# PV of both halves in the next step, and preparation in small pieces: attention and two expert layers on one core

## The chip, the cores and the metric

The program runs on one core of a Trainium2 chip. The metric is the device time of one execution in microseconds (us); 1592.23 us is the median of three runs of the kernel before (1590.58 to 1593.88). The engines are named as the profile names them: PE (TensorE's matmuls), PEld (its weight loads), DVE (the vector engine), ACT (the scalar engine), POOL and SP (which issues nearly all DMAs).

## The reference

Three parts follow one another. Attention: 8 batches, 8 heads, 576 tokens, head size 64, with a mask by blocks of 64:

```python
scores = 1/np.sqrt(64) * (q @ k.transpose(0, 1, 3, 2))
scores = np.where(block_i >= block_j, scores, -1e9)      # blocks of 64 tokens
attn = exp(scores - max); attn = attn / (attn.sum(-1) + 1e-09)
x = (attn @ v) as 4608 tokens x 512
```

Then a gated layer, `h = ((x @ w1) * (x @ w2)) @ w3 @ w_out`, with w1 and w2 of 512 x 1024, w3 of 1024 x 1024, w_out of 1024 x 512. Then routing: `logits = h @ w_gate` for 8 experts, each token given in the order of all logits to the best expert that still has room (576 tokens each), and `relu(h @ w1[e]) @ w2[e]` of its expert. The gated layer's w1, w2, w3 and w_out arrive as float64 and are decoded to float32 on the chip (`decode`); the rest is float32.

## The kernel before

Products are made in float16 pairs: a value is scaled by a power of two and split into a high and a low half (`split`: ACT writes the high half, DVE the low one), and three of the four products are summed in PSUM (`PRODUCTS`). The scale comes from a sum of squares (`ssq` on ACT), summed over partitions by a matmul with ones (`total`, PE), and a few tiny DVE operations (`pow2`).

The attention stage is a loop over 32 steps (`step`), one for each pair of heads n of batch n // 4. A step has four score tiles in PSUM (`s_tiles`): `last` (64 query tokens of both heads), and `rows` for 128-token blocks 3, 2 with 0, and 1. For each, PE makes the scores into S; DVE takes the row maximum (nb); ACT takes the exponential (E) with its sum; DVE takes the reciprocal; ACT or DVE writes the high half of P and DVE the low half (`finish`). `last` and block 3 fill one SBUF tile of P (13 blocks wide, PT13 when transposed), the rest another (12 wide, PT12). When such a tile is full, `transP` issues two DMA transposes on SP, one a half, into one buffer each. `pv(n, part)` multiplies the transposed tile with v: part 0 is PT13 (54 matmuls), part 1 PT12 (36). Both use the single PSUM bank named PV, which ACT and DVE evict into xT (`pv`'s last lines); the w34 products of the weights use the same bank.

Into the list of a step's work are woven the step's fills (`interleave`): the decoding, scaling and splitting of w1 and w2 (`do_w`, steps 1 to 7), the chunks of w_out (steps 8 to 11) with `wo_split` and `wo_dot` (step 12), w3 and `w34` (steps 14 to 31), and from step 5 on four `moe_unit`s a step. A unit is 24 matmuls of 288 columns into two `ab` banks: ACT evicts the first as a_sb, DVE multiplies it with the second to g, and SP stores two of them (gd).

The preparation of a step's inputs stands between its score tiles: at odd n `prep_qk` (squares of q and k, `total`, scale, both splits, and the copy q4 for `last`) and the load of the next q and k; at n divisible by 4 `scale_v` (squares of a batch's v); at even n `prep_v` (the split of v for two steps, 1280 columns).

The code gives only an order of priority. The framework's scheduler sets the order on each engine: it goes through the list by priority and by when its own model finds an instruction's inputs ready. From the route on (`manual_schedule`) the order of PE, ACT and POOL is written out. So the same lines may come out elsewhere in an engine's stream than they stand in the code. In the sections below, a tile's name with a number is one buffer of that name.

Of the kernel before, what the change touches and what calls it, by code (L numbers as in the profile page):

```python
# [27 lines left out]
OSTEP = 8  # L28
# [31 lines left out]
def moe_kernel(ctx, tc, q, k, v, moe_w1, moe_w2, moe_w3, moe_w_out, w_gate, ew1, ew2, out):  # L60
# [14 lines left out]
    def pow2(pool, m, name, TB=TB, inv=None, **kw):  # L75
        n = m.shape[-1]
        t = pool.tile([P, 3, n], I32, name=name, **kw)
        nc.vector.tensor_scalar(t[:, 0], m.bitcast(I32), 24, 23, op0=ALU.logical_shift_right,
                                op1=ALU.logical_shift_left)
        nc.vector.tensor_scalar(t[:, 1], t[:, 0], -1.0, float((189 + TB) << 23), op0=ALU.mult, op1=ALU.add)  # L80
        if inv is not None:
            nc.gpsimd.tensor_scalar(inv.bitcast(I32), t[:, 0], float((65 - TB) << 23), 0.0, op0=ALU.add, op1=ALU.add)
            return t[:, 1].bitcast(F32), None
        nc.vector.tensor_scalar(t[:, 2], t[:, 0], float((65 - TB) << 23), None, op0=ALU.add)
        return t[:, 1].bitcast(F32), t[:, 2].bitcast(F32)
# [31 lines left out]
    def split(hi, lo, x, s):  # L117
        nc.scalar.activation(hi, x, AF.Copy, scale=s)
        nc.vector.scalar_tensor_tensor(lo, x, s, hi, op0=ALU.mult, op1=ALU.subtract)
# [5 lines left out]
    def ssq(x, dst, junk):  # L125
        nc.scalar.activation(junk, x, AF.Square, accum_out=dst)
# [8 lines left out]
    def load_v(b):  # L135
        nc.sync.dma_start(v32, v[b])

    def scale_v(b):
        m = sm.tile([P, 3], F32, name="vm")
        vhl[4 * b] = c2.tile([P, 2, 4, 5, D], F16, name="v16")  # L140
        j = vhl[4 * b].rearrange("p z h j d -> p (z h) j d")
        for x in range(3):
            ssq(v32[:, :, 2 * x:min(2 * x + 2, 5), :], m[:, x:x + 1], j[:, :, 2 * x:min(2 * x + 2, 5), :])
        m2 = total(m)
        m3 = sm.tile([P, 1], F32, name="vm3")
        nc.vector.tensor_reduce(m3, m2, axis=AX.X, op=ALU.add)
        sv[b] = pow2(sm, m3, "vp")

    def prep_v(n):
        b, hp = divmod(n, NP)  # L150
        vt = vhl[n] if n % 4 == 0 else c2.tile([P, 2, 4, 5, D], F16, name="v16")
        split(vt[:, 0], vt[:, 1], v32[:, 2 * hp:2 * hp + 4], sv[b][0])
        vhl[n], vhl[n + 1] = vt[:, :, 0:2], vt[:, :, 2:4]

    def scale_x(b):
        r = mo.tile([P, 8], F32, name="vr", bufs=2)
# [9 lines left out]
    def unscale(b, f):  # L166
        nc.vector.tensor_scalar(iv[b][:, f], iw12[:, f], ivs[b], ivs[b], op0=ALU.mult, op1=ALU.mult)

    def prep_qk(g):
        n0, n1 = GROUPS[g]  # L170
        t, w = qk32.pop(g), n1 - n0
        m = sm.tile([P, 2], F32, name="qm")
        T = c2.tile([P, 2, 2, 2, S], F16, name="qkT")
        for z in range(2):
            ssq(t[:, z, :w], m[:, z:z + 1], T[:, z, 1, :w])
        s, e = pow2(sm, total(m), "qp")
        c = sm.tile([P, 2], F32, name="cc")
        for z, f in enumerate((1.0, -1.0)):
            nc.vector.scalar_tensor_tensor(c[:, z:z + 1], e[:, 0:1], f * 0.125, e[:, 1:2],
                                           op0=ALU.mult, op1=ALU.mult)  # L180
        for z in range(2):
            split(T[:, z, 0, :w], T[:, z, 1, :w], t[:, z, :w], s[:, z:z + 1])
        for hh in range(2):
            r = slice(64 * hh, 64 * hh + 64)
            nc.vector.tensor_copy(q4[r, :, n0 % 2:n0 % 2 + w, r], T[r, 0, :, :w, 512:])
        for n in range(n0, n1):
            qkT[n] = T[:, 0, :, n - n0], T[:, 1, :, n - n0], q4[:, :, n % 2], c

    PRODUCTS = ((0, 0), (0, 1), (1, 0))

# [209 lines left out]
    def total(m):  # L400
        n = m.shape[-1]
        p = ps_l.tile([P, 512], F32, name="lgp")
        nc.tensor.matmul(p[:, :n], ones, m, start=True, stop=True)
        return p[:, :n]

    es_w = ExitStack()
    stg_w = es_w.enter_context(tc.tile_pool(name="stg_w", bufs=2))

    def prep_w(n, f):
        w = stg_w.tile([P, 512], F32, name="wd")  # L410
        decode((n, f), w)
        m = sm.tile([P, 1], F32, name="wm")
        t = w16[n][f].rearrange("p z c f -> p z (c f)")
        ssq(w, m, t[:, 1])
        e = scaled(w, total(m), t[:, 0], t[:, 1], "wp")
        nc.vector.tensor_copy(iw[n][:, f:f + 1], e)
        if n == "w2":
            nc.vector.scalar_tensor_tensor(iw12[:, f:f + 1], iw["w1"][:, f:f + 1], 2.0 ** 15, e, op0=ALU.mult, op1=ALU.mult)
# [28 lines left out]
    def wo_split():  # L447
        m2 = total(wo["m"])
        m3 = sm.tile([P, 1], F32, name="wom3", bufs=1)
        nc.vector.tensor_reduce(m3, m2, axis=AX.X, op=ALU.add)  # L450
        s, e = pow2(sm, m3, "wop")
        wo["e"] = e
        t = wo["t"]
        for c in range(8):
            w = wo["w"][:, c]
            split(t[:, c, 0], t[:, c, 1], w, s)
        wo["wg"], wo["eg"] = hilo(wo["g"], 4, "wgx")

    def wo_dot():
        wo["stack"].close()  # L460
# [76 lines left out]
            else:  # L537
                load_raw(x, wi[x[0]][x[1]])

    def do_w(n, f):  # L540
        prep_w(n, f)
        next_load()

    def do(f, *a):
        f(*a)
        next_load()
# [3 lines left out]
    load_v(0)  # L550
    prep_qk(0)
    prep_qk(1)
    for _ in range(2):
        next_load()
    scale_v(0)
# [4 lines left out]
    for n, m in WSTEP.items():  # L560
        for _ in range(m):
            x = next(ws)
            add(n, do_w, *x)
    for c in range(8):
        add(OSTEP + c // 2, do, wo_chunk, c)
    add(OSTEP + 4, wo_split)
    add(OSTEP + 4, wo_dot)
    for f in range(8):
        a, b_ = S3 + int(R3 * f), S3 + int(R3 * f + R3 / 2)
        add(a, do, w3_chunk, f, 0)  # L570
# [22 lines left out]
    def step(n):  # L593
        ops = []
        if n < NS:
            a, b_, c, d = s_tiles(n)
            pre = []
            if n % 2:
                g = first.get(n + 1)
                if g is not None:  # L600
                    pre.append(lambda: prep_qk(g))
                    if g + 1 < len(GROUPS):
                        pre.append(lambda: load_qk(g + 1))
            elif n == 0:
                pre.append(lambda: load_qk(2))
            if n % 4 == 0 and n:
                pre.append(lambda: scale_v(n // 4))
            if n % 2 == 0 and n:
                pre.append(lambda: prep_v(n))
            if n % 4 == 3 and n // 4 + 1 < B:  # L610
                pre.append(lambda: load_v(n // 4 + 1))
            ops += [a, lambda: (b_(), transP(n, 0))]
            ops += pre
            ops += [c, lambda: (d(), transP(n, 1))]
            if n:
                ops.insert(2, lambda: pv(n - 1, 1))
            ops.append(lambda: pv(n, 0))
        elif n == NS:
            ops.append(lambda: pv(n - 1, 1))
        if n % 4 == 0 and 0 < n <= NS:  # L620
            ops.append(lambda: scale_x(n // 4 - 1))
        interleave(ops, fills[n])
# [538 lines left out]
```

## Time and profile before

| | |
|---|---|
| median of three runs | 1592.23 us (1590.58 to 1593.88) |
| profiled execution, its time | 1593.24 us |
| profiled execution, span from first to last instruction | 1591.5 us |
| mean granted clock of TensorE | 0.944 |
| PE busy | 1376.4 us |
| DVE busy | 1024.5 us |
| ACT busy | 891.7 us |

Busy is the time in which an engine has at least one instruction under way. The granted clock is the share of TensorE's 2.4 GHz that the throttle let through; 0.5 is its lower level of 1.2 GHz. A row of waits names who waited, for whom, and the time in total, how often, and the longest. In a row of the timeline, the square bracket holds the idle time of the engine ahead of the row and what ended it.

### The profile page before, as it was taken

How to read it: one execution, taken by the hardware profiler on the slowest of the kernel's cores; microseconds unless marked ns; L12 is line 12 of the kernel's file. 1: busy time of each engine (PE TensorE's matmuls, PEld its weight loads, DVE VectorE, ACT ScalarE, POOL GpSimd, SP SyncE). 2: the span in 40 equal slices, each digit the busy share in tenths (PEclk: the TensorE clock that was granted, in tenths of full speed). 3: DMA queues.
4: the chain of work that ended last, by engine and by line, in shares of the span. 5: the costliest groups of instructions: out<-in, count | busy, mean ns of one | idle time of the engine just before them, and what ended most of it. 6: DMA issues, size and time to landing. Idle time of an engine off the chain costs nothing. (4 is left out here: it accounts for less than half of the span.)

```text
span 1591.5 us, 32778 instructions
## 1 busy us (share of the span) xinstructions
PE 1376.4 (86%) x12811; PEld 942.3 (59%) x12811; DVE 1024.5 (64%) x3068; ACT 891.7 (56%) x2121; POOL 98.0 (6%) x136
## 2 busy tenths in 40 slices
PE   3558887978998999999999888888768999989997
PEld 2335565656666666666666665656555656556663
DVE  8898888777788787874224888878743353343610
ACT  8887977577677677754322333353314564555721
POOL 0000000000000000100200000000023121200101
PEclk9557999999999999999999999989879999999999
DMA  8758796886768676469964434333258663642200
GB/s 266 185 146 173 187 221 119 186 186 136 168 161 202 155 183 120 93 119 249 295 202 148 127 101 133 100 113 100 100 112 187 177 201 133 123 175 74 80 27 34
DMA packets 379659, 238.57 MB, mean 150 GB/s; under 512 B 261232, under 2 KB 344688, under 8 KB 378480
## 3 DMA queue, kind: packets, MB, share of 16 engines
q1 hardware_dynamic: 372064, 215.47, 52.9%
q0 software_dynamic: 5760, 18.90, 4.0%
q10 hardware_dynamic: 1680, 2.11, 0.6%
q8 instruction: 100, 1.64, 0.4%
q14 instruction: 55, 0.45, 0.1%
HBM read 132.61 MB, written 39.86 MB: 108 GB/s over the span
## 5 line engine op out<-in xcount | busy, mean ns | idle before, releaser
L301 PE MATMUL ab<-xT,w1h 128*128 128x288 f16 x1536 | 223.0, 295 | 11.5 <-ACT a_sb L306 11.3
L301 PE MATMUL ab<-xT,w2h 128*128 128x288 f16 x1536 | 215.4, 289 | 7.7 <-DVE g L311 3.6
L1079 PE MATMUL pe<-xT,ewa 128*128 128x288 f16 (+2 forms) x1728 | 198.6, 279 | 16.8 <-DMA xT<-xg 9.4
L1079 PEld LDWEIGHTS <-ewa 128*128 128x128 f16 x1728 | 160.7, 101 | 53.5 <-DVE sc L1057 9.5
L1096 PE MATMUL pe<-ewb,h 128*128 128x512 f16 (+1 forms) x960 | 189.1, 379 | 0.0
L301 PEld LDWEIGHTS <-w1h 128*128 128x128 f16 x1536 | 147.1, 101 | 66.3 <-issue 24.4
L221 ACT ACTIVATE E<-S,nb,cc 128x128 f32<-128x128 f32 (+4 forms) x288 | 181.1, 637 | 2.8 <-DVE P L232 0.9
L301 PEld LDWEIGHTS <-w2h 128*128 128x128 f16 x1536 | 146.4, 99 | 53.3 <-issue 13.5
L232 DVE SCALAR_TENSOR_TENSOR P<-E,rr,P 128x128 f16<-128x128 f32 (+4 forms) x288 | 155.7, 573 | 13.7 <-ACT P L231 11.9
L276 PE MATMUL PV<-PT,v 128*64 128x128 f16 (+1 forms) x2880 | 100.7, 225 | 53.0 <-DMA PT<-P 45.7
L1096 PEld LDWEIGHTS <-h 128*128 128x128 f16 (+1 forms) x960 | 85.3, 101 | 99.2 <-issue 2.6
L276 PEld LDWEIGHTS <-v 128*64 128x64 f16 x2880 | 86.5, 120 | 75.8 <-issue 49.7
L1082 DVE SCALAR_TENSOR_TENSOR h<-pe,h 128x288 f16<-128x288 f32 (+2 forms) x144 | 57.2, 419 | 106.9 <-ACT h L1081 106.6
L922 PE MATMUL px<-W34l,gh 128*128 128x512 f32 x288 | 123.0, 427 | 0.0
L922 PE MATMUL px<-W34h,gh 128*128 128x512 f32 x288 | 122.0, 424 | 0.0
L937 ACT ACTIVATE gh<-g 128x1024 fp32r<-128x1024 f32 x36 | 38.1, 1059 | 149.8 <-PE px L922 142.6
L922 PE MATMUL px<-W34h,gl 128*128 128x512 f32 x288 | 121.9, 423 | 0.0
L311 DVE SCALAR_TENSOR_TENSOR g<-ab,vr,a_sb 128x288 f32<-128x288 f32 x124 | 63.5, 512 | 83.6 <-PE ab L301 73.6
L1081 ACT ACTIVATE h<-pe 128x288 f16<-128x288 f32 (+2 forms) x144 | 52.5, 380 | 111.7 <-PE pe L1079 110.1
L200 PE MATMUL S<-qkT 64*128 64x512 f16 (+3 forms) x768 | 83.7, 324 | 27.1 <-ACT E L221 26.3
L213 DVE TENSOR_REDUCE nb<-S 128x2 f32<-128x1024 f32 (+3 forms) x128 | 101.2, 814 | 7.5 <-PE S L204 7.4
L231 ACT ACTIVATE P<-E,rr 128x128 f16<-128x128 f32 (+3 forms) x176 | 97.2, 603 | 12.9 <-DVE rr L225 11.4
(279 smaller groups left out, 2173.3 us busy)
## 6 DMA issues: line engine op xcount, KB each, us to landing
g<-gd SPq DMA_DIRECT2D x36, 512.0 KB, 3.9
gd<-g SPq DMA_DIRECT2D x62, 288.0 KB, 2.9
g<-gd SPq DMA_DIRECT2D x15, 1152.0 KB, 7.2
raw<-in_moe_w_dram SPq DMA_DIRECT2D x32, 512.0 KB, 4.8
esa<-in_moe_w_dram SPq DMA_DIRECT2D x8, 2048.0 KB, 9.2
esb<-in_moe_w_dram SPq DMA_DIRECT2D x8, 2048.0 KB, 9.5
v<-in_v_dram SPq DMA_DIRECT2D x8, 1280.0 KB, 6.5
xr<-row SPq DMA_DIRECT2D x36, 256.5 KB, 3.0
```

What stands on the lines that cost most here:

```text
L200: nc.tensor.matmul(ps[:, hh, o:o + N], tq[r, a, m * P:m * P + P], tk[r, b, :N], start=a + b == 0, stop=False)
L213: nc.vector.tensor_reduce(nb[:, 0, k_:k_ + 2], ps[:, :, o:o + N], axis=AX.X, op=ALU.max)
L221: nc.scalar.activation(ef[:, a], pf_[:, a], AF.Exp, bias=nb[:, 1, x:x + 1], scale=c[:, 0:1], accum_out=sums[:, x:x + 1])
L231: nc.scalar.activation(hi, ef[:, at[x]], AF.Copy, scale=r[:, 1, x:x + 1])
L232: nc.vector.scalar_tensor_tensor(lo, ef[:, at[x]], r[:, 1, x:x + 1], hi, op0=ALU.mult, op1=ALU.subtract)
L276: nc.tensor.matmul(ps[hh * 64:hh * 64 + 64, c0:c0 + w], vt[:, zv, hh, j, :], s, start=z == 0 and j == 0, stop=z == 2 and j == nj - 1)
L301: nc.tensor.matmul(p[:, :288], w[:, zw, cc, :], x[:, zx, cc, c0:c0 + 288], start=first, stop=cc == 3 and zw == 1)
L311: nc.vector.scalar_tensor_tensor(g, ps["w2"][:, :288], iv[b][:, f:f + 1], a, op0=ALU.mult, op1=ALU.mult)
L922: nc.tensor.matmul(p, gh[a][:, f], W34[b][:, f], start=f == 0 and a + b == 0, stop=f == 7 and a == 1)
L1079: nc.tensor.matmul(p[:, :n], w1[:, a, cc, f * P:(f + 1) * P], t[:, 4 * b + cc, x], start=cc == 0 and a + b == 0, stop=cc == 3 and a == 1)
L1082: nc.vector.scalar_tensor_tensor(h[:, 1, f, x], p[:, :n], 0.0, h[:, 0, f, x], op0=ALU.max, op1=ALU.subtract)
L1096: nc.tensor.matmul(p[r0:r1], h[:, a, f, k_ * P + r0:k_ * P + r1], EW[e, "b"][0][:, b, f], start=f == 0 and a + b == 0, stop=f == 7 and a == 1)
```

## The change

Both halves of pv(n-1) are handed over in step n, the first behind `last`, the second behind the third score tile; before, the first half stood at the end of step n-1 and the second behind the second tile of step n. `prep_qk` is cut into squares and scale (at the even step before) and two splits (at the odd step). v is split for each step (640 columns) into four smaller buffers instead of for two steps (1280 columns) into two. The decoding of w1 and w2 (`dec_w`) and their split (`prep_w`) are two fills, and the next raw load is issued behind the first. The eight splits of w_out are fills of their own, in steps 12 and 13, and `wo_dot` moves to step 13. All pieces are dealt out between the step's score tiles.

```diff
     def scale_v(b):
         m = sm.tile([P, 3], F32, name="vm")
-        vhl[4 * b] = c2.tile([P, 2, 4, 5, D], F16, name="v16")
+        vhl[4 * b] = c2.tile([P, 2, 2, 5, D], F16, name="v16", bufs=4)
...
     def prep_v(n):
         b, hp = divmod(n, NP)
-        vt = vhl[n] if n % 4 == 0 else c2.tile([P, 2, 4, 5, D], F16, name="v16")
-        split(vt[:, 0], vt[:, 1], v32[:, 2 * hp:2 * hp + 4], sv[b][0])
-        vhl[n], vhl[n + 1] = vt[:, :, 0:2], vt[:, :, 2:4]
+        if hp:
+            vhl[n] = c2.tile([P, 2, 2, 5, D], F16, name="v16", bufs=4)
+        split(vhl[n][:, 0], vhl[n][:, 1], v32[:, 2 * hp:2 * hp + 2], sv[b][0])
...
+    pq = {}
+
+    def qk_scale(g):
+        n0, n1 = GROUPS[g]
+        w = n1 - n0
+
+        def sq(z):
+            if z == 0:
+                pq[g] = sm.tile([P, 2], F32, name="qm"), c2.tile([P, 2, 2, 2, S], F16, name="qkT")
+            m, T = pq[g]
+            ssq(qk32[g][:, z, :w], m[:, z:z + 1], T[:, z, 1, :w])
+
+        def fin():
+            m, T = pq[g]
+            s, e = pow2(sm, total(m), "qp")
+            c = sm.tile([P, 2], F32, name="cc")
+            for z, f in enumerate((1.0, -1.0)):
+                nc.vector.scalar_tensor_tensor(c[:, z:z + 1], e[:, 0:1], f * 0.125, e[:, 1:2],
+                                               op0=ALU.mult, op1=ALU.mult)
+            pq[g] = s, c, T
+
+        return [lambda: sq(0), lambda: sq(1), fin]
+
+    def qk_split(g):
+        n0, n1 = GROUPS[g]
+        w = n1 - n0
+
+        def sp(z):
+            s, c, T = pq[g]
+            split(T[:, z, 0, :w], T[:, z, 1, :w], qk32[g][:, z, :w], s[:, z:z + 1])
+            if z == 0:
+                for hh in range(2):
+                    r = slice(64 * hh, 64 * hh + 64)
+                    nc.vector.tensor_copy(q4[r, :, n0 % 2:n0 % 2 + w, r], T[r, 0, :, :w, 512:])
+                return
+            del qk32[g]
+            for n in range(n0, n1):
+                qkT[n] = T[:, 0, :, n - n0], T[:, 1, :, n - n0], q4[:, :, n % 2], c
+
+        return [lambda: sp(0), lambda: sp(1)]
+
     def prep_qk(g):
...
+        for f in qk_scale(g) + qk_split(g):
+            f()
...
+    def dec_w(n, f):
+        wd[n, f] = stg_w.tile([P, 512], F32, name="wd")
+        decode((n, f), wd[n, f])
+        next_load()
+
     def prep_w(n, f):
-        w = stg_w.tile([P, 512], F32, name="wd")
-        decode((n, f), w)
+        w = wd.pop((n, f))
...
-        t = wo["t"]
-        for c in range(8):
-            w = wo["w"][:, c]
-            split(t[:, c, 0], t[:, c, 1], w, s)
+        wo["s"] = s
         wo["wg"], wo["eg"] = hilo(wo["g"], 4, "wgx")
+
+    def wo_half(c):
+        split(wo["t"][:, c, 0], wo["t"][:, c, 1], wo["w"][:, c], wo["s"])
...
     add(OSTEP + 4, wo_split)
-    add(OSTEP + 4, wo_dot)
+    for c in range(8):
+        add(OSTEP + 4 + c // 5, wo_half, c)
+    add(OSTEP + 5, wo_dot)
...
-            pre = []
+            u = []
             if n % 2:
                 g = first.get(n + 1)
                 if g is not None:
-                    pre.append(lambda: prep_qk(g))
-                    if g + 1 < len(GROUPS):
-                        pre.append(lambda: load_qk(g + 1))
-            elif n == 0:
-                pre.append(lambda: load_qk(2))
+                    u += qk_split(g)
+                    u.append(lambda: load_qk(g + 1) if g + 1 < len(GROUPS) else None)
+            else:
+                g = first.get(n + 2)
+                if g is not None and n:
+                    u += qk_scale(g)
             if n % 4 == 0 and n:
-                pre.append(lambda: scale_v(n // 4))
-            if n % 2 == 0 and n:
-                pre.append(lambda: prep_v(n))
+                u.insert(0, lambda: scale_v(n // 4))
+            if n:
+                u.append(lambda: prep_v(n))
             if n % 4 == 3 and n // 4 + 1 < B:
-                pre.append(lambda: load_v(n // 4 + 1))
-            ops += [a, lambda: (b_(), transP(n, 0))]
-            ops += pre
-            ops += [c, lambda: (d(), transP(n, 1))]
+                u.append(lambda: load_v(n // 4 + 1))
+            k_ = (len(u) + 1) // 2
+            ops.append(a)
             if n:
-                ops.insert(2, lambda: pv(n - 1, 1))
-            ops.append(lambda: pv(n, 0))
+                ops.append(lambda: pv(n - 1, 0))
+            ops.append(lambda: (b_(), transP(n, 0)))
+            ops += u[:k_]
+            ops.append(c)
+            if n:
+                ops.append(lambda: pv(n - 1, 1))
+            ops += u[k_:]
+            ops.append(lambda: (d(), transP(n, 1)))
+            if n == 0:
+                ops += qk_scale(2)
         elif n == NS:
-            ops.append(lambda: pv(n - 1, 1))
+            ops += [lambda: pv(n - 1, 0), lambda: pv(n - 1, 1)]
```

Two places show what the scheduler makes of it. The first is PE at the start of step 11: L239 is its `last` tile, L276 the first half of PV of step 10, which reads PT13. Before:

```order
L239 MATMUL S_3704<-qkT_3133,q4_111 128x512
L239 LDWEIGHTS q4_111
L239 MATMUL S_3704<-qkT_3133,q4_111 128x64
L276 LDWEIGHTS v16_3500
L276 MATMUL PV_3616<-PT13_3396,v16_3500 64x128
L276 LDWEIGHTS v16_3500
L276 MATMUL PV_3616<-PT13_3396,v16_3500 64x128
```

The same place of the changed program, where L266 is `last` and L328 the matmul of a unit; PV of step 10 (L303) follows behind twelve of them:

```order
L266 MATMUL S_3675<-qkT_2746,q4_111 128x512
L266 LDWEIGHTS q4_111
L266 MATMUL S_3675<-qkT_2746,q4_111 128x64
L328 LDWEIGHTS w1h7_77
L328 MATMUL ab_3645<-xT_1404,w1h7_77 128x288
L328 LDWEIGHTS w1h7_77
L328 MATMUL ab_3645<-xT_1404,w1h7_77 128x288
```

In both programs this half stands behind `last` of the next step; half a unit has come between.

The second is ACT where w_out is split: L118 with `wo` is the scaling of one of its eight chunks, L306 the eviction a_sb of a unit. Before:

```order
L217 ACTIVATE nb<-nb,cc 128x2
L231 ACTIVATE P_119<-E,rr 128x576
L221 ACTIVATE E,sums<-S,nb,cc 128x512 x2
L118 ACTIVATE wo_2780<-wo_2778,wop 128x512 x8
L306 ACTIVATE a_sb<-ab 128x288
L231 ACTIVATE P_119<-E,rr 128x512 x2
```

The same chunks in the changed program, where a_sb is L333:

```order
L333 ACTIVATE a_sb<-ab 128x288
L118 ACTIVATE wo_2755<-wo_2753,wop 128x512 x3
L258 ACTIVATE P_120<-E,rr 128x128 x2
L126 ACTIVATE v_4181,vm<-v_122 128x1024
L244 ACTIVATE nb<-nb,cc 128x1
L307 ACTIVATE xT<-PV 128x192
L118 ACTIVATE wgxh<-wg,wgxp 128x4x8
L118 ACTIVATE wo_2755<-wo_2753,wop 128x512 x5
L333 ACTIVATE a_sb<-ab 128x288
```

Three chunks stand ahead of a square of v, an eviction of PV and others, and five behind them, with a_sb directly after.

## Rows read from the trace of the kernel before

**Rows 1.** The page: busy us, share of the span and instructions of each engine.

```profile
PE 1376.4 (86%) x12811; PEld 942.3 (59%) x12811; DVE 1024.5 (64%) x3068; ACT 891.7 (56%) x2121; POOL 98.0 (6%) x136
```

**Rows 2.** Windows: stretch, length, busy us by engine (instructions), clock, DMA share, GB/s.

```profile
40.00:130.00 90.00, 50.25 (x562) 34.39 (x562) 81.83 (x236) 75.43 (x184) 0.00 (x0) 0.54 0.70 163
130.00:280.00 150.00, 121.75 (x1423) 87.60 (x1422) 130.17 (x332) 121.65 (x305) 0.00 (x0) 0.93 0.78 178
250.00:260.00 10.00, 5.09 (x73) 3.89 (x71) 4.49 (x13) 7.30 (x24) 0.00 (x0) 0.77 0.90 173
280.00:520.00 240.00, 212.88 (x2538) 150.34 (x2538) 186.79 (x473) 170.99 (x420) 0.00 (x0) 0.98 0.76 172
520.00:760.00 240.00, 225.96 (x2596) 156.10 (x2594) 175.34 (x445) 156.39 (x392) 5.92 (x13) 1.00 0.69 157
760.00:1592.00 832.00, 749.80 (x5565) 504.00 (x5564) 418.11 (x1495) 332.60 (x747) 90.42 (x112) 0.96 0.43 129
```

**Rows 3.** Waits from 130 to 280 us: us in total, times, longest.

```profile
PE PV L276 <- DMA PT<-P: 11.8, 9, 3.7
...
PE ab L301 <- ACT a_sb L306: 8.4, 5, 2.9
```

**Rows 4.** Waits from 280 to 520 us.

```profile
PE PV L276 <- DMA PT<-P: 11.4, 11, 3.1
```

**Rows 5.** Waits from 520 to 760 us.

```profile
PE PV L276 <- DMA PT<-P: 6.8, 7, 1.8
...
PE PV L276 <- DVE xT L281: 1.4, 1, 1.4
```

**Rows 6.** Waits from 40 to 130 us.

```profile
PE S L200 <- ACT E L221: 18.5, 8, 4.8
PE PV L276 <- DMA PT<-P: 14.5, 7, 4.7
```

**Rows 7.** Timeline of PE, 250 to 262 us: start, us, instruction, idle before.

```profile
249.78 1.27 PE L301 MATMUL ab<-xT,w2h 128*128 128x288 f16 x9
251.63 0.90 PE L239 MATMUL S<-qkT,q 128*128 128x512 f16 x6 [0.58 <-ACT E L221]
256.17 0.64 PE L276 MATMUL PV<-PT,v 128*64 128x128 f16 x8 [3.65 <-DMA PT<-P]
```

**Rows 8.** DMA issues: median us from issue to landing.

```profile
PT<-P SPq DMA_TRANSPOSE x128, 4.3
```

**Rows 9.** Timeline, 674 to 684 us: one handover of the PV bank.

```profile
675.32 1.20 PE L276 MATMUL PV<-PT,v 128*64 128x128 f16 x36
...
680.63 0.48 ACT L280 ACTIVATE xT<-PV 128x384 f16<-128x384 f32 x1
...
682.54 0.55 DVE L281 SCALAR_TENSOR_TENSOR xT<-PV,xT 128x384 f16<-128x384 f32 x1
...
683.15 1.05 PE L276 MATMUL PV<-PT,v 128*64 128x128 f16 x36 [1.37 <-DVE xT L281]
```

**Rows 10.** Lines: out and in, count, busy us, mean ns, idle before.

```profile
L119 DVE SCALAR_TENSOR_TENSOR v<-v,vp,v 128x1280 f16<-128x1280 f32 x16 | 24.6, 1543 | 1.1 <-ACT v L118 1.1
L118 ACT ACTIVATE v<-v,vp 128x1280 f16<-128x1280 f32 x16 | 21.7, 1361 | 0.8 <-DVE vp L84 0.8
L119 DVE SCALAR_TENSOR_TENSOR wo<-wo,wop,wo 128x512 f16<-128x512 f32 x8 | 5.6, 743 | 0.2 <-ACT wo L118 0.2
...
L118 ACT ACTIVATE wo<-wo,wop 128x512 f16<-128x512 f32 x8 | 5.0, 707 | 0.0
```

**Rows 11.** Timeline of PE at the split of w_out.

```profile
273.81 1.63 PE L301 MATMUL ab<-xT,w1h 128*128 128x288 f16 x12 [2.88 <-ACT a_sb L306]
276.94 1.63 PE L301 MATMUL ab<-xT,w2h 128*128 128x288 f16 x12 [1.50 <-DVE wgxp L80]
```

**Rows 12.** Timeline of ACT at the same place.

```profile
268.48 4.99 ACT L118 ACTIVATE wo<-wo,wop 128x512 f16<-128x512 f32 x8
273.37 0.39 ACT L306 ACTIVATE a_sb<-ab 128x288 f32<-128x288 f32 x1
```

More of the change, by code (lines that the diff above doesn't have):

```diff
@@ L139, in scale_v @@
         m = sm.tile([P, 3], F32, name="vm")
-        vhl[4 * b] = c2.tile([P, 2, 4, 5, D], F16, name="v16")
-        j = vhl[4 * b].rearrange("p z h j d -> p (z h) j d")
+        vhl[4 * b] = c2.tile([P, 2, 2, 5, D], F16, name="v16", bufs=4)
+        j = vhl[4 * b].rearrange("p z h j d -> p (z h j d)")
         for x in range(3):
-            ssq(v32[:, :, 2 * x:min(2 * x + 2, 5), :], m[:, x:x + 1], j[:, :, 2 * x:min(2 * x + 2, 5), :])
+            w = min(2, 5 - 2 * x)
+            ssq(v32[:, :, 2 * x:2 * x + w, :], m[:, x:x + 1],
+                j[:, :H * w * D].rearrange("p (h j d) -> p h j d", h=H, j=w))
         m2 = total(m)
@@ L167, in unscale @@
         nc.vector.tensor_scalar(iv[b][:, f], iw12[:, f], ivs[b], ivs[b], op0=ALU.mult, op1=ALU.mult)
-    def prep_qk(g):
[L170 to L187, printed above, removed]
+    pq = {}
@@ L407, in moe_kernel @@
     stg_w = es_w.enter_context(tc.tile_pool(name="stg_w", bufs=2))
+    wd = {}
+    def dec_w(n, f):
+        wd[n, f] = stg_w.tile([P, 512], F32, name="wd")
+        decode((n, f), wd[n, f])
+        next_load()
     def prep_w(n, f):
-        w = stg_w.tile([P, 512], F32, name="wd")
-        decode((n, f), w)
+        w = wd.pop((n, f))
         m = sm.tile([P, 1], F32, name="wm")
@@ L538, in next_load @@
                 load_raw(x, wi[x[0]][x[1]])
-    def do_w(n, f):
-        prep_w(n, f)
-        next_load()
     def do(f, *a):
@@ L552, in moe_kernel @@
     prep_qk(1)
+    load_qk(2)
     for _ in range(2):
@@ L562, in moe_kernel @@
             x = next(ws)
-            add(n, do_w, *x)
+            add(n, dec_w, *x)
+            add(n, prep_w, *x)
     for c in range(8):
```

## Prediction

> **What bounds the kernel now.** I read the page's busy shares first, then a table of windows, then the waits of TensorE window by window, and last the timeline at the places that the edits touch.
>
> The page says 86% busy for PE, 64% for DVE, 56% for ACT [rows 1], but these shares mix two programs. All edits lie in the attention stage, which fills the first 760 us; from there to the end the two programs issue the same work, and TensorE's order is the same word for word over its last 4,668 matmuls. So the question is what 760 us become.
>
> The windows cut that stage into parts with different limits [rows 2]. From 40 to 130 us DVE is busy 81.8 of 90 us and ACT 75.4, while PE has 50.3 and a granted clock of 0.54: the vector and scalar engines set the pace, PE is starved. From 130 to 280 us DVE is still the fullest engine (130.2 of 150), with PE at 121.8 and ACT at 121.7. From 280 us PE takes over: 212.9 of 240, then 226.0 of 240. What PE leaves idle is therefore worth 0 before 130 us, little before 280, and nearly its full length after: 27.1 us in 280 to 520 and 14.0 in 520 to 760.
>
> The waits say what ends that idleness. PE's PV matmuls wait for their transposed P (DMA PT<-P) for 11.8, 11.4 and 6.8 us in the three windows from 130 us on [rows 3 to 5], the largest single cause; the next is the `ab` matmul that waits for the eviction of its bank (a_sb), 8.4 us in the first of them [rows 3]. In 40 to 130 us the same DMA costs PE 14.5 us and the scores' wait for the exponential 18.5 [rows 6], but DVE is full there, so I count none of it.
>
> **The change part by part.**
>
> *PV one step later.* In the code pv(n-1, 0) now stands behind the first score tile of step n; it stood at the end of step n-1. In the instruction stream this is far smaller, since the scheduler already pushed PV back. Counted in the order of PE before: 17 of 32 first halves start behind the next step's `last` tile already; after: 26. Of the second halves 26 start behind the next step's third score tile before, 30 after. What counts is how much matmul work stands between the last score tile that feeds a half and that half's first matmul, since the softmax and two transposes run beside it. With about 1.6 us for each dozen `ab` matmuls and 0.9 us for a `last` tile (1.27 us for nine, 0.90 [rows 7]), I get under 13 us for 16 of the 54 halves from step 5 on before, and for 7 after; from step 12 on (280 us) 15 of 40 before and 6 after, but 1 of 14 in both programs for steps 5 to 11. The wait of 3.65 us at 256 us [rows 7] is one such place: the new order puts 12 `ab` matmuls ahead of it, which covers 1.6 us of 3.65. From the 18.2 us of such waits behind 280 us [rows 4, 5] I take half: **-9 us**. Bounds: 0 (all come back as other waits) and -30.0 (all waits from 130 us on go). Before 280 us I take 0, since the count of short distances doesn't fall there and DVE is the limit. The DMAs themselves don't change; on SP each transpose of PT13 now also stands behind pv(n-1, 0), which reads the single buffer. In 27 of 32 steps that half starts before the scores of the tile that the new P waits for, so PT13 is read out long before; the SP queue gets no new wait of weight, and what stands behind it (raw, qk, gd) none either. Cost 0, bounded by one landing of 4.3 us [rows 8] in each of the 5 others: 0 to +21.
>
> *One bank for all PV halves.* Both halves and the w34 products use one PSUM bank. Of its 71 handovers 36 had under 6 us of matmuls between them, now 48; under 3 us 4, now 8. The eviction is 0.5 us on ACT and 0.55 on DVE when both come at once, but at 675 us the product ended at 676.5, ACT came to it at 680.6, DVE at 682.5, ended at 683.1, and the next PV waited 1.37 us [rows 9]. I put 0.5 us on each of the 4 closest new ones: **+2 us**, between 0 and 12 handovers x 1.6 us = +19 (6.6 us eviction in that row less a mean gap of about 5).
>
> *v in 32 pieces instead of 16.* The widths 512 and 1280 give the price of a piece [rows 10]: ACT 707 and 1361 ns, so 0.85 ns a column and 816 ns at 640, twice that less 1361 is 0.27 us; DVE 743 and 1543 ns, so 876 at 640 and 0.21 us more for two. 16 extra pieces are 4.3 us of ACT and 3.4 of DVE. About 6 fall into the first 280 us, where DVE is full: **+1.3 us**; the rest lies beside PE (DVE 78% and 73% busy there [rows 2]), at 0, or +2.1 if that cover is gone. The Trainium skill's page "Perfetto Trace Analysis", section "Optimizing Scalar/DVE Operations", speaks against the edit: larger operations are better where the engine is saturated, at about 60 ns of DVE and 93 ns of ACT an instruction; by these figures, an estimate, the extra pieces cost 1.0 and 1.5 us, a third of what the rows say, and the sum would be 0.9 us lower. The same section holds that breaking up helps where the engine is not saturated, which is the state behind 280 us.
>
> *w_out in 8 pieces.* Before, eight scalings stand in a row on ACT, 268.5 to 273.4 us; a_sb waits behind them, and PE idles 2.88 us and then 1.50 for DVE's half [rows 11, 12]. In the new order they come as 3 and 5 with five rows of softmax and others between, and a_sb stands directly behind the five. So 5/8 of the burst stays: of 4.4 us I take **-2 us**, between 0 and -4.4.
>
> *q, k and the weights.* Squares, scale and split of q and k go from one burst at an odd step to three places; the same instructions, with no DMA more or less (426 on SP in both). In ACT's order the two squares and the two splits still stand in pairs mostly. The raw load is issued behind the decode instead of behind the split: at most ahead of where it was. I take 0, with -5 and +5 as bounds, from the 8.4 us of a_sb waits [rows 3] of which part stands behind such pairs.
>
> Sum: -9 + 2 + 1.3 - 2 = -7.7 us. The profiled execution took 1593.24 us (1.7 around its span); 1593.24 - 7.7 = 1585.5. That execution lies 1.0 above the median of 1592.23, inside the spread of the runs, so I name **1585 us**.
>
> **The rivals.**
>
> *A. Nothing measurable.* The scheduler had already done most of this: PV stands one step later in over half of the cases. If the cadence is set by the sum of DVE and ACT work, a wait that goes at PV comes back at `ab` or at the scores. For it: DVE and ACT have the same instructions but 16 each, and DVE is at 87 to 91% to 280 us. Against it: PE is at 94% behind 520 us, so there it is PE. Time: 1593.2 - 18.2 x 0.1 + 1.3 = 1592.7.
>
> *B. Much more.* All PT waits behind 280 us go (18.2), the w_out stall as a whole (4.4), and the clock stays up. The clock fell to 0.77 in the window with the 3.65 us stall, and over 130 to 280 us it is 0.93 [rows 2]; 7% of 121.8 us busy and 2% of 212.9 are 12.8 us, of which half may come back. 1593.2 - 18.2 - 4.4 - 6.4 + 1.3 = 1565.5. The Trainium skill, "TensorE: Matmul & The Clock Gate", section "HAM oscillation", has this mechanism: short bursts of matmuls with waits between them drop back to the slow clock again and again. By that rule each wait costs more than its length, which the 0.77 row agrees with. Against B: most of the lost clock lies at 130 to 150 us, where PE only begins to have work.
>
> *C. Slower: the single PV bank.* Halves that are packed closer behind each other and behind w34 find the bank not evicted, since ACT and DVE serve it late [rows 9]. At its price of 12 x 1.6 = 19.2 instead of my 2: 1593.2 - 9 - 2 + 1.3 + 19.2 = 1602.7. It makes the kernel slower from 1.1 us a handover on. For it: the handover at 683 us waited although 6.6 us lay between [rows 9]. Against it: that is PE's only such wait in 520 to 760 us [rows 5].
>
> **How the numbers follow.** Forecast (-3.2 to -18): 0.44; A: 0.18; B (under -18): 0.16; C: 0.22. A measurement of this kernel can't tell 0.2% (3.2 us) from no change. Faster is the forecast and B: 0.60; same is A: 0.18; slower is C: 0.22. The range for 8 in 10 leaves out the better half of B and the worse part of C: **1563 to 1603**; the forecast's own is 1575 to 1590.
>
> **What would show it.** Right: PV's wait for DMA PT falls from 18.2 us to some 9 in 280 to 760 us, PE's busy share there rises from 91% to about 93%, and the stage ends some 8 us earlier, with the rest of equal length. The a_sb wait at the w_out split is down to about 2 us. B shows as a clock of 0.97 or more in 130 to 280 us; C as PV matmuls that wait for DVE xT for over 10 us in total; A as a smaller PT wait with a larger wait for a_sb, g or the exponential. The forecast is wrong if the first 280 us, where I count +1.3 alone, move by more than 5 us either way, or if the part behind the attention stage changes length.

## The result and the profile after

The changed kernel takes **1571.16 us** (median of 7 runs, 1565.79 to 1578.51), the kernel before on the same chip 1591.63 us (7 runs, 1582.03 to 1593.88). The ratio is 0.9887, with a 95% interval of 0.9855 to 0.9920: faster by 20 us. The forecast was faster by 7.7 us, at 1585.

The profiled execution of the changed kernel is the slowest of its seven, 1578.51 us with a span of 1576.8. Between the two traces the gain is therefore 14.7 us; the other 5.8 us of the medians' difference are in no trace. The traces show where the 14.7 us come from.

First the page of after, answering [rows 1]:

```profile
PE 1375.8 (87%) x12811; PEld 940.0 (60%) x12811; DVE 1025.6 (65%) x3084; ACT 893.5 (57%) x2137; POOL 98.5 (6%) x136
```

All busy times moved by at most 2.3 us. So no engine got less work; PE waits less. The windows of after, against [rows 2]:

```profile
40.00:130.00 90.00, 48.48 (x571) 32.15 (x571) 78.13 (x223) 74.16 (x182) 0.00 (x0) 0.66 0.70 167
130.00:280.00 150.00, 124.89 (x1444) 88.84 (x1440) 136.83 (x356) 123.84 (x309) 0.00 (x0) 0.94 0.81 187
250.00:260.00 10.00, 7.66 (x75) 5.35 (x74) 8.12 (x24) 5.76 (x14) 0.00 (x0) 0.83 1.19 207
280.00:520.00 240.00, 221.69 (x2644) 157.19 (x2644) 194.53 (x499) 183.35 (x457) 0.00 (x0) 0.98 0.78 176
520.00:760.00 240.00, 227.76 (x2604) 155.48 (x2603) 168.45 (x428) 148.14 (x374) 6.22 (x14) 0.99 0.73 163
760.00:1577.00 817.00, 737.39 (x5422) 496.55 (x5420) 415.00 (x1485) 329.15 (x741) 90.71 (x112) 0.96 0.43 127
```

From 280 to 520 us PE now does 2644 matmuls instead of 2538, and is idle 18.3 us instead of 27.1. The attention stage with the units of the gated layer ends at 839.3 us instead of 852.7. Two windows from 40 us to that end, of before and then of after, say that this is all idle time:

```profile
40.00:852.70 812.70, 702.11 (x7880) 490.08 (x7883) 591.53 (x1521) 547.11 (x1346) 15.53 (x18) 0.93 0.73 172
```

```profile
40.00:839.30 799.30, 702.12 (x7883) 487.27 (x7886) 593.24 (x1536) 549.44 (x1359) 15.82 (x19) 0.94 0.75 176
```

PE's busy time is equal to 0.01 us; its idle time is 110.6 us before and 97.2 after, 13.4 us less. One more cut says when, again before and then after:

```profile
250.00:520.00 270.00, 233.59 (x2764) 165.40 (x2762) 209.53 (x529) 194.68 (x478) 0.00 (x0) 0.97 0.75 165
```

```profile
250.00:520.00 270.00, 247.03 (x2933) 174.94 (x2932) 219.11 (x559) 202.37 (x504) 0.00 (x0) 0.97 0.79 174
```

Idle time there falls from 36.4 to 23.0 us: 13.4 us, the whole of it (before 250 us it grows by 3.3, behind 520 us it falls by 3.2).

Which waits? First from 40 to 130 us, against [rows 6], then 130 to 280 [rows 3], 280 to 520 [rows 4] and 520 to 760 us [rows 5], all of after:

```profile
PE PV L303 <- DMA PT<-P: 10.2, 7, 5.0
PE PV L303 <- DVE rr L251: 7.0, 1, 7.0
PE S L266 <- ACT E L248: 6.4, 2, 4.1
...
PE S L227 <- ACT E L248: 3.6, 4, 1.7
PE PV L303 <- DVE xT L308: 3.0, 2, 1.6
```

```profile
PE ab L328 <- ACT a_sb L333: 9.2, 5, 3.2
PE PV L303 <- DMA PT<-P: 8.4, 7, 2.3
```

```profile
PE PV L303 <- DMA PT<-P: 10.1, 6, 4.0
```

```profile
PE PV L303 <- DMA PT<-P: 3.3, 2, 2.4
...
PE PV L303 <- DVE xT L308: 0.8, 1, 0.8
```

PV's wait for the transposed P falls by 1.3 us in 280 to 520 and by 3.5 in 520 to 760: 18.2 to 13.4, not to 9. The early rows show a trade: the block scores' wait for E (L200 in before, L227 here) goes from 18.5 to 3.6 us and PV's for PT from 14.5 to 10.2, but PV now waits 7.0 us for DVE's `rr` (the reciprocals) and `last` 6.4 for E, and other waits of a few us beside them; at 250 us nothing of it is left. The rest of the gain is spread over many waits: from 280 to 520 us those of `ab` for a_sb go from 3.6 to 0.9 us, and waits for w3 of 2.8 us (DVE's w3f) and 2.2 us (a DMA) are gone.

At the split of w_out, ACT's timeline and then PE's, against [rows 12] and [rows 11]:

```profile
237.44 1.96 ACT L118 ACTIVATE wo<-wo,wop 128x512 f16<-128x512 f32 x3
...
241.50 3.18 ACT L118 ACTIVATE wo<-wo,wop 128x512 f16<-128x512 f32 x5
244.57 0.41 ACT L333 ACTIVATE a_sb<-ab 128x288 f32<-128x288 f32 x1
```

```profile
240.16 1.63 PE L328 MATMUL ab<-xT,w2h 128*128 128x288 f16 x12 [0.92 <-DVE g L338]
245.03 3.04 PE L328 MATMUL ab<-xT,w1h 128*128 128x288 f16 x12 [3.23 <-ACT a_sb L333]
```

The eight stand as 3 and 5, as forecast, but PE still loses 4.15 us beside them (4.38 before), and the whole thing happens 31 us earlier. The split did not shrink the stall; the new order moved it. It even costs more: the twelve matmuls behind the wait of 3.23 us took 3.04 us, where the twelve ahead of it took 1.63. PE's granted clock had been 1.00 from 240 to 242 us; behind the wait, from 246 to 248 us, it was at about its lower level. Beside the two waits of before, from 270 to 278 us, it stayed at 1.00. The two stretches, of after and then of before:

```profile
246.00:248.00 2.00, 2.00 (x11) 1.35 (x9) 2.00 (x5) 2.00 (x6) 0.00 (x0) 0.51 1.03 197
```

```profile
270.00:278.00 8.00, 3.62 (x38) 2.75 (x35) 8.00 (x16) 8.00 (x17) 0.00 (x0) 1.00 0.24 46
```

With the 1.41 us of slower matmuls the place costs 5.6 us instead of 4.4.

The pieces of v, by lines, DVE and ACT, against [rows 10]:

```profile
L118 ACT ACTIVATE v<-v,vp 128x640 f16<-128x640 f32 x32 | 25.2, 823 | 0.5 <-DVE vp L80 0.5
```

```profile
L119 DVE SCALAR_TENSOR_TENSOR v<-v,vp,v 128x640 f16<-128x640 f32 x32 | 27.5, 879 | 1.0 <-ACT v L118 1.0
```

A piece takes 823 and 879 ns (816 and 876 forecast), and the lines' busy time grows by 3.5 and 2.9 us (4.3 and 3.4 forecast). The price of the edit's own instructions was read about rightly; it was not what decided.

### The profile page after: what moved, and what is told of

Its sections match the earlier page's. It is cut to its first block, busy times and chain, and to the rows that moved or that the text cites. A ratio compares the mean times of both kernels' runs of the same rounds, so it can differ in the third digit from the quotient of the medians.

```text
span 1576.8 us, 32791 instructions
## 1 busy us (share of the span) xinstructions
PE 1375.8 (87%) x12811; PEld 940.0 (60%) x12811; DVE 1025.6 (65%) x3084; ACT 893.5 (57%) x2137; POOL 98.5 (6%) x136
## 5 line engine op out<-in xcount | busy, mean ns | idle before, releaser
L328 PE MATMUL ab<-xT,w1h 128*128 128x288 f16 x1536 | 220.4, 293 | 14.3 <-ACT a_sb L333 10.9
L328 PE MATMUL ab<-xT,w2h 128*128 128x288 f16 x1536 | 220.8, 293 | 2.5 <-DVE g L338 1.5
L1120 PE MATMUL pe<-xT,ewa 128*128 128x288 f16 (+2 forms) x1728 | 198.9, 280 | 14.7 <-DMA xT<-xg 9.8
L328 PEld LDWEIGHTS <-w1h 128*128 128x128 f16 x1536 | 146.3, 100 | 66.1 <-issue 24.3
L328 PEld LDWEIGHTS <-w2h 128*128 128x128 f16 x1536 | 147.8, 100 | 57.6 <-issue 15.0
L259 DVE SCALAR_TENSOR_TENSOR P<-E,rr,P 128x512 f16<-128x512 f32 (+4 forms) x288 | 156.6, 575 | 14.2 <-ACT P L258 12.1
L303 PE MATMUL PV<-PT,v 128*64 128x128 f16 (+1 forms) x2880 | 102.2, 224 | 47.6 <-DMA PT<-P 33.4
L303 PEld LDWEIGHTS <-v 128*64 128x64 f16 x2880 | 84.5, 118 | 73.3 <-issue 37.8
L333 ACT ACTIVATE a_sb<-ab 128x288 f32<-128x288 f32 x128 | 52.1, 407 | 84.6 <-PE ab L328 80.4
```

Source lines behind the costliest of these rows:

```text
L259: nc.vector.scalar_tensor_tensor(lo, ef[:, at[x]], r[:, 1, x:x + 1], hi, op0=ALU.mult, op1=ALU.subtract)
L303: nc.tensor.matmul(ps[hh * 64:hh * 64 + 64, c0:c0 + w], vt[:, zv, hh, j, :], s, start=z == 0 and j == 0, stop=z == 2 and j == nj - 1)
L328: nc.tensor.matmul(p[:, :288], w[:, zw, cc, :], x[:, zx, cc, c0:c0 + 288], start=first, stop=cc == 3 and zw == 1)
L333: nc.scalar.activation(a, p[:, :288], AF.Copy, scale=2.0 ** -15)
L1120: nc.tensor.matmul(p[:, :n], w1[:, a, cc, f * P:(f + 1) * P], t[:, 4 * b + cc, x], start=cc == 0 and a + b == 0, stop=cc == 3 and a == 1)
```

## The experiments

Each kernel has 5 to 12 runs, against the kernel before on the same chip (1590.91 us for the first four, 1591.48 for the next four, 1593.57 for the last four). Idle is PE's idle time from 250 to 520 us in the profiled execution, which is 270 less its busy time there.

| kernel | median us | ratio, 95% interval | idle |
|---|---|---|---|
| before | 1591 to 1594 | 1 | 36.4 |
| after | 1571.2 | 0.9887 (0.9855 to 0.9920) | 23.0 |
| PV handover alone | 1582.4 | 0.9946 (0.9925 to 0.9967) | 21.9 |
| all pieces, PV as before | 1566.2 | 0.9848 (0.9824 to 0.9872) | 20.3 |
| after, one piece shifted | 1573.1 | 0.9885 (0.9860 to 0.9909) | 21.2 |
| before, preparation behind the third tile | 1592.9 | 1.0009 (0.9984 to 1.0035) | 26.6 |
| w_out's edit alone | 1574.2 | 0.9898 (0.9869 to 0.9926) | 20.6 |
| q and k alone | 1576.3 | 0.9906 (0.9879 to 0.9933) | 29.9 |
| v alone | 1570.4 | 0.9870 (0.9839 to 0.9901) | 21.0 |
| weights alone | 1578.2 | 0.9916 (0.9886 to 0.9947) | 18.7 |
| w_out's product a step later, nothing cut | 1582.0 | 0.9932 (0.9909 to 0.9955) | 27.6 |
| w_out a step later, nothing cut | 1584.6 | 0.9950 (0.9931 to 0.9970) | 26.0 |
| fills one place earlier, nothing cut | 1575.3 | 0.9893 (0.9866 to 0.9921) | 25.6 |
| all pieces but v's | 1581.3 | 0.9926 (0.9900 to 0.9953) | 27.3 |

**PV or the pieces?** The theory of the prediction is that PV's later handover carries the gain; the rival, that the pieces do. Two kernels do one part each. The first is before with

```diff
             ops += [a, ...]
+            if n: ops.append(lambda: pv(n - 1, 0))   # behind `last`
...
+            if n: ops.append(lambda: pv(n - 1, 1))   # behind the third tile
-            ops.append(lambda: pv(n, 0))
```

> Only the PV halves are handed over one step later, all preparation stays in its old bursts. By the theory that PE's waits for the transposed P carry the change, it keeps most of the gain: 10 to 16 us less than before, and PV's wait for DMA PT in steps 5 to 31 falls from 27.7 us to about 20. By the rival that the spread of the preparation carries it, 0 to 5 us less. By the second rival, that any other order moves the time as much by chance, it may lie anywhere within 15 us of before.

It gains 8.6 us, between the two forecasts. Its waits for PT, in 280 to 520 and then in 520 to 760 us:

```profile
PE PV L276 <- DMA PT<-P: 3.2, 5, 1.0
```

```profile
PE PV L276 <- DMA PT<-P: 7.0, 6, 2.5
```

That is 10.2 us instead of 18.2: alone, the handover does to these waits what the prediction said of it, and the time is near the forecast's -9 + 2. That the waits gave the 8.6 us is not shown: from 118 to 760 us they fall by 15.5 us (30.0 to 14.5), almost twice the gain, and orders with no such aim gain as much below. The second is after with PV put back:

```diff
             ops.append(a)
-            if n: ops.append(lambda: pv(n - 1, 0))
...
+            ops.append(lambda: pv(n, 0))
```

> All preparation in small pieces, the PV halves handed over as before. By the theory that the PV waits carry the change, within 5 us of before, with PV's wait for DMA PT in steps 5 to 31 at about 27 us still. By the rival, 12 to 20 us less than before.

It gains 24.2 us by the ratio, more than the rival's 12 to 20 and at least as much as the whole change, while its waits for PT from 280 to 760 us are not smaller than those of before:

```profile
PE PV L303 <- DMA PT<-P: 18.4, 23, 2.7
```

So the theory that PT waits carry the gain falls. The pieces are enough without PV; whether PV adds or costs something on top can't be told, since the intervals of this kernel and of after overlap narrowly.

**Is it the place of one burst?** After with the middle cut shifted by one piece, and before with its unbroken preparation moved behind the third tile:

```diff
-            k_ = (len(u) + 1) // 2
+            k_ = len(u) // 2
```

> The changed kernel with one piece of a step's preparation moved from ahead of the third score tile to behind it wherever their number is odd: a move that neither theory gives a price. If the gain has a cause it stays: 13 to 23 us less than before. If orders differ by chance, it comes out 5 us or more away from the changed kernel (-20 us).

```diff
-            ops += pre
-            ops += [c, lambda: (d(), transP(n, 1))]
+            ops.append(c)
+            ops += pre
+            ops.append(lambda: (d(), transP(n, 1)))
```

> The kernel before with a step's burst of preparation moved as a whole behind the third score tile. Neither theory gives it a price of more than 3 us: halves of PV with little matmul work ahead of them are 13 instead of 16, so 0 to 3 us less than before. If orders differ by chance, 5 us or more to either side.

The first stands where after stands, the second where before stands. So not every new order moves the time. Moving the burst alone gives nothing, though its idle time from 250 to 520 us is less (26.6): its attention stage ended at 852.0 us all the same.

**Which piece?** Four kernels are before with one piece of the change each: w_out's eight fills and the later product; squares and scale of q and k a step ahead; v for each step; decoding and split of the weights as two fills.

> The kernel before with the w_out split alone in eight pieces over steps 12 and 13, and the product with w_gate behind it a step later. Preparation in pieces gave -24 us as a whole. If the one long burst of ACT and DVE at 268 us is what it removes, this alone gives -6 to -12 us, made between units 24 and 48. If every burst gives its share, -2 to -5 us.

> The kernel before with q and k prepared in pieces alone: squares and scale one step early, the two splits as pieces of their own. If every burst gives its share, this is the largest, since it recurs in 15 steps: -6 to -12 us, spread over steps 4 to 31. If the w_out burst or the weights carry the change, within 4 us of before.

> The kernel before with v split for each step instead of for two steps alone, in the same place of a step. 16 pieces more on ACT and DVE cost 4.3 and 3.4 us of their time: by the price of a piece +1 to +3 us; if shorter pieces let ACT serve PE's banks sooner, -2 to -5 us.

> The kernel before with decoding and split of w1 and w2 as two fills and the next raw load behind the first, alone. It acts in steps 1 to 7, where DVE and ACT are full with the same work: 0 to -3 us by that. If the earlier load is what helps, ACT's wait for the raw DMA falls from 22 us by half and the time by 5 to 10 us, all of it before 180 us.

```diff
 # w_out
-        for c in range(8):
...
-            split(t[:, c, 0], t[:, c, 1], w, s)
...
+    for c in range(8):
+        add(OSTEP + 4 + c // 5, wo_half, c)
+    add(OSTEP + 5, wo_dot)
 # q and k, at odd and at even n
-                    pre.append(lambda: prep_qk(g))
+                    pre += qk_split(g)
...
+                    pre += qk_scale(g)
 # v
-            if n % 2 == 0 and n:
+            if n:
                 pre.append(lambda: prep_v(n))
...
 # weights
-            add(n, do_w, *x)
+            add(n, dec_w, *x)
+            add(n, prep_w, *x)
```

Each alone gains 13 to 21 us: 15.0 for q and k, 13.4 for the weights, 16.2 for w_out, 20.7 for v (each 1591.48 times one minus its ratio). Their sum is 65 us, where all together give 24. None of the four is small, all gain more than any of their forecasts allowed, and they don't add. In the weights' kernel ACT's idle time ahead of the decoding, nearly all of it for the raw DMA, fell from 27.1 to 18.1 us, but the gain does not lie before 180 us, as that forecast had it: the ninth unit begins at 181.1 us instead of 174.5. Only v's edit cuts instructions: it has 16 more on DVE and on ACT (3084 and 2137). The other three have the instructions of before, in number and in shape (3068 and 2121), and change their order alone.

The trace of w_out's kernel says more. PE's order is that of before, matmul for matmul, until 239 us. Then ACT and PE:

```profile
241.08 5.00 ACT L118 ACTIVATE wo<-wo,wop 128x512 f16<-128x512 f32 x8
```

```profile
243.44 0.38 PE L403 MATMUL lgp<-wgxm,ones 128*128 128x1 f32 x2
245.77 1.63 PE L301 MATMUL ab<-xT,w2h 128*128 128x288 f16 x12 [1.95 <-DVE g L311]
```

The eight splits are fills of their own in the code, but the scheduler put them side by side again: a row of eight, 5.00 us, as before (4.99 [rows 12]). **Nothing was broken up, and the kernel is 16 us faster.** What changed is where the row stands (27 us earlier) and everything behind it. In the weights' kernel the row stands where it stood, at 270.65 us for 5.00 us, and beside it PE has one wait of 1.00, for a transpose:

```profile
274.07 0.38 PE L403 MATMUL lgp<-wgxm,ones 128*128 128x1 f32 x2
275.45 0.25 PE L276 MATMUL PV<-PT,v 128*64 128x128 f16 x2 [1.00 <-DMA PT<-P]
```

So the row by itself does not make the stall of 4.4 us; what stands beside it in before's order has a part in it. From this came a new theory: the change acts by the order. The scheduler goes through one list by priority, so an edit anywhere re-sorts all that follows, and before's order is a poor one between 250 and 290 us. There PE's timeline, beside the waits in [rows 7] and [rows 11], has these:

```profile
257.48 1.86 PE L276 MATMUL PV<-PT,v 128*64 128x128 f16 x46 [0.67 <-DMA PT<-P]
...
283.94 0.44 PE L276 MATMUL PV<-PT,v 128*64 128x128 f16 x9 [1.67 <-DMA PT<-P]
...
289.60 1.63 PE L301 MATMUL ab<-xT,w1h 128*128 128x288 f16 x12 [1.13 <-ACT a_sb L306]
```

Together 3.65 + 0.67 + 2.88 + 1.50 + 1.67 + 1.13 = 11.5 us in 40.

**Order without pieces.** Three kernels change before's order and cut nothing; a fourth takes one piece out of the fine version.

```diff
-    add(OSTEP + 4, wo_dot)                 # product a step later
+    add(OSTEP + 5, wo_dot)
```

> The kernel before with one number changed: the product of w_out with the gate's weights one step later; w_out is still scaled in one row of eight. It is what remains of the w_out edit (14 to 20 us faster alone) when its pieces are taken away. Small pieces as the cause: nothing left, 1588 to 1594 us. The order as the cause (any edit that shifts the fills against the score tiles between 250 and 300 us breaks up the stretch in which TensorE idled 12 us): 1572 to 1583 us, with TensorE's idle time from 250 to 520 us down from 36 to below 27 us.

```diff
-OSTEP = 8                                  # all of w_out a step later
+OSTEP = 9
```

> The kernel before with the whole chain of w_out (loads, squares, the row of eight, the product) one step later; nothing is cut into pieces, no instruction more or less. Small pieces as the cause: the row of eight only stalls a step later, 1588 to 1594 us. The order as the cause: 1572 to 1583 us, TensorE's idle time from 250 to 520 us below 27 us.

```diff
     for ia, f in enumerate(a):              # interleave: fills one place earlier
-        f()
         while ib < nb and (ib + 1) * na <= (ia + 1) * nb:
             b[ib]()
             ib += 1
+        f()
```

> The kernel before with every fill of a step (weights, expert units) put ahead of the score tile behind which it stood; no piece is cut. It moves the order of all 32 steps. Small pieces as the cause: 1588 to 1596 us. The order as the cause, if the order of before is an unlucky one: 1572 to 1583 us; if orders scatter to both sides: anywhere from 1575 to 1600 us.

```diff
-            if n:                            # all pieces, but v for two steps
+            if n % 2 == 0 and n:
                 u.append(lambda: prep_v(n))
...
```

> The kernel with all preparation in pieces and PV as before (1566 us), but v in 16 pieces as before. Gains that add: v alone gave 21 of the 24 us, so 1583 to 1588 us. Gains that all remove the same idle time (v, w_out, q and k, weights each gave 13 to 21 us alone): 1566 to 1575 us, and TensorE's idle time from 250 to 520 us stays at 18 to 23 us.

All three orders are faster than before: by 10.8, 8.0 and 17.1 us. The first changes one number, and its order on PE is that of before until 278 us; its idle time missed the bound of 27 us by 0.6. The second ended 1.6 us above the forecast of the order theory, and its gain stands on the medians alone: in its profiled execution, the slowest of six (1590.83 us), the attention stage ends at 856.7 us, later than in that of before, although its idle time is down to 26.0. The third, with every piece whole and PV as it was, has a ratio of 0.9893; the whole change has 0.9887. Its PE from 250 to 300 us, and then that of before:

```profile
250.00:300.00 50.00, 46.05 (x601) 33.85 (x599) 38.17 (x94) 38.04 (x95) 0.00 (x0) 1.00 0.73 148
```

```profile
250.00:300.00 50.00, 37.79 (x425) 27.10 (x423) 36.03 (x92) 33.84 (x86) 0.00 (x0) 0.93 0.66 133
```

601 matmuls instead of 425, idle 4.0 us instead of 12.2. `interleave` also deals out the expert layer's weights, so this edit reaches past the attention stage; but of the 15.4 us between the two spans, 12.4 lie ahead of the last unit's end (840.3 us instead of 852.7). So order alone gives a gain of the size of the change.

The fourth came out between the two forecasts, nearer to gains that add, and its idle time of 27.3 us contradicts the theory that all pieces remove the same idle time. But gains that add fail as well: three pieces together gain 11.8 us, no more than any one of the three by itself (13.4 to 16.2), where their sum is 44.6.

**What is settled and what is not.** Shown: the kernel's time depends on the order by up to 17 us without any edit that costs or saves work. Nine of the kernels issue the same instructions as before, the edits of w_out, of q and k and of the weights among them; they gain -1 to 17 us, 11 in the mean (mean ratio 0.9931). Likely, not shown: v's cut adds something of its own. The four kernels with v in 32 pieces gain 18 to 24 us by their ratios (0.9848 to 0.9887). In both pairs that differ in v's edit alone it gains: before and v alone 0.9870; all pieces but v's and all pieces 0.9926 and 0.9848, with intervals apart. But each edit of v is a new order too, and the interval of the best of the nine (0.9866 to 0.9921) covers three of these four ratios. w_out's edit with its eight fills and without them, 0.9898 against 0.9932, has intervals that overlap, and there the row was not broken up. Open: what makes one order better than another. Idle time from 250 to 520 us is lower in every kernel than in before, but doesn't rank them, as the shifted burst shows. The end of the attention stage in the traces goes better with the ratios: 834.6 us with all pieces and PV as before, 835.7 to 845.7 in ten others, 852.0 with the shifted burst and 852.7 in before; only w_out a step later (856.7) does not fit.

## Why the prediction was right and wrong

The direction was right, and 1571 us lies in the range; the size was not. That was in part luck, since the -9 on which the direction rested is not what the gain needs: with the pieces alone and PV as before the kernel is 24.2 us faster. 1571 is below the forecast's own range (1575 to 1590), and rival B, whose time of 1565.5 is nearest, named other causes than those measured: its clock of 0.97 in 130 to 280 us is 0.94. What the prediction held against B was misread: from 130 to 150 us the clock is 0.83, but from 160 to 280 us, six times as long, it is 0.94, so the greater part of the lost clock lies later (0.06 of 120 us against 0.17 of 20). Point by point:

- **PV one step later, -9.** The waits fell by 4.8 us in 280 to 760 us, not by 9; alone they fell by 8.0. For the edit by itself the waits and the time have the forecast's size, though it is not shown that one made the other; in the company of the others a good part of the fall in waits is gone, and there the handover adds no gain (0.9887 with it, 0.9848 without). The bound on the single PT13 buffer needs no correction, since no wait of weight on SP's side appeared.
- **One PV bank, +2; rival C.** PV's waits for xT are 3.0 us in 40 to 130 us, and 0.8 in 520 to 760, where it was 1.4 [rows 5]. C needed over 10; it fell, and of the +2 nothing shows from 280 us on.
- **v in 32 pieces, +1.3.** The price of a piece was right to 1%, and the sign of the effect wrong: v alone gains 20.7 us. The Trainium skill's page "Perfetto Trace Analysis", section "Optimizing Scalar/DVE Operations", says that breaking up instructions may let work end sooner where the engines aren't saturated but cause idle time elsewhere. Here the runs agree in direction. How much of the 20.7 us is that and how much the new order, the runs don't separate. On the price the same section has 93 and 60 ns an instruction as busy time, about twice that as the profile's latency; the lines show 0.22 us of ACT and 0.18 of DVE for each extra piece, nearer to the doubled figures.
- **w_out in 8 pieces, -2.** The stall lost 0.2 us, not 2, and came 31 us earlier. The reading that a shorter row means a shorter stall failed: PE's waits beside the row of eight are 4.4, 2.0 and 1.0 us in three kernels that all have it whole.
- **q, k and the weights, 0 with bounds of -5 and +5.** With v's, this is the step that failed most: alone they gain 15.0 and 13.4 us. "The same instructions, with no DMA more or less" was true and no argument: these are edits of order alone, as are the three of the last group, which gain 8 to 17 us.
- **Rival A**, that the scheduler had already done most of it, fell: it had 1592.7 us, and only a part of the waits came back, as PV's 7.0 us for `rr`.
- **The marks that were named.** PE's busy share from 280 to 760 us is 93.6% (93 forecast) and the part behind the attention stage keeps its length (730.1 us from the last unit to the last matmul before, 728.7 after). The stage ends 13.4 us earlier, not 8. On the first 280 us, which were allowed 5 us, the traces are divided. The 25th unit began at 273.8 us before and begins at 267.7 after, 6.1 us earlier, but `last` of step 11 begins at 259.8 instead of 251.6, later. From 40 to 280 us PE does 2015 matmuls instead of 1985 (the first two windows of each table), which at a unit's price (24 in 3.3 us) are an estimated 4 us.

The fault lies under all these terms. The sum prices each edit where it stands and takes the rest of the program as fixed. The prediction had seen that the scheduler moves PV away from its place in the code, and did not conclude that it moves everything else as well. A term for it, from the kernels above with the same instructions, would have been +1 to -17 us, larger than any term of the sum. Whether the 20 us are such an order alone or in part v's cut stays open.

## What to carry to other kernels

Where a scheduler decides the order, a change has two effects: its own, which can be priced from rows, and a new draw of the order, which can't. Measure the second before explaining the first: run two or three neutral changes of order, and call a cause shown only if it exceeds their spread. Where PE idles for a quarter of 40 us, trying other orders is itself a cheap optimisation: one number changed gave 11 us, and the best version here, all pieces with PV as before, 1566.17 us.

## What was not expected of the hardware

The same program varies more than the medians suggest: the changed kernel took 1565.8 to 1578.5 us in seven executions, the kernel before 1582.0 to 1593.9. Part of it lies where PE's order is the same. From the expert layer's first matmul to its last these are four traces: before, after, all pieces with PV as before, and the shifted burst:

```profile
1180.93:1582.76 401.83, 387.09 (x2714) 248.74 (x2714) 139.67 (x349) 197.23 (x475) 65.99 (x67) 0.98 0.45 125
```

```profile
1167.11:1568.02 400.91, 387.46 (x2714) 249.55 (x2714) 139.94 (x349) 196.87 (x475) 66.42 (x67) 0.98 0.45 125
```

```profile
1161.68:1553.49 391.81, 383.77 (x2714) 247.23 (x2714) 139.80 (x349) 196.64 (x475) 66.44 (x67) 0.99 0.45 128
```

```profile
1182.22:1574.83 392.61, 382.67 (x2714) 245.86 (x2714) 139.57 (x349) 196.68 (x475) 66.60 (x67) 0.99 0.45 128
```

The same 2714 matmuls take 401.8, 400.9, 391.8 and 392.6 us. The last two kernels are the fastest and the slowest by their ratios, so a short layer is no mark of a fast kernel. That it changes from one execution to the next is likely, not shown, since each kernel has one trace. So a single trace places gains to some 10 us in that part, and the kernel with all pieces and PV as before owes part of its short profiled execution to a stage that its edit doesn't touch.
